# Three schedule changes around the start of the expert stage: a list prepared later in one part, one key chunk moved to VectorE, two rank products a gap later

## Chip, core and metric

The kernel runs on one NeuronCore of a Trainium2 chip. The metric is the device time of one execution in microseconds. Before the change three runs took 671.76 us (median), 670.19 and 672.02 us.

## What is computed

Three layers follow each other. Clustered attention (2 batches, 8 heads, 768 positions, 64 per head): a query sees only the keys of its own cluster, a key's or query's cluster being the nearest of 16 centroids. Its output, 1536 tokens of 512, goes through a mixture of 8 experts with two experts per token, and that through a soft mixture.

```python
mask = q_assign[:, :, :, None] == k_assign[:, :, None, :]
scores = np.where(mask, scale * np.matmul(q, k.transpose(0, 1, 3, 2)), -1e9)
attn = np.exp(scores - max) ; attn /= attn.sum(-1) + 1e-9 ; x = attn @ v
# experts: noisy top 2 of 8 per token
h = np.maximum(x[mask] @ w1[e], 0.0)            # 512 -> 1024
out[mask] += top2_w[mask, k, None] * (h @ w2[e])  # 1024 -> 512
# soft mixture: 32 slots, softmax over tokens in, over slots out
```

## The kernel before

Instructions are issued by hand in an order that Python loops write out; each engine then runs its own instructions in that order and waits for semaphores. Attention runs over 8 pairs of heads (NP = 8), each pair over two query halves `qh` and six key chunks `kc`. For each chunk TensorE makes the scores, ScalarE the exponentials `pt`, TensorE multiplies with the values. The denominators need the sum of the six `pt` tiles; `add` splits these sums: the first `n` chunks go to GpSimd (`psa`), the rest to VectorE (`psb`). `n` is 6 for pair 0, 4 below pair `MASKED` and 3 from it on.

The token routing is done by `gate`, called for the first 6 blocks of 128 tokens and then for two groups of 3. A gate is a list of some 40 small operations, most on VectorE, a few on ScalarE, and `rank`: a few small matmuls that number the tokens of each expert, followed by two VectorE operations that read the result. The integers in the list are pauses. `gap(s, n)` takes up to `n` operations off the list `todo`; an integer ends the gap, and counts down by one for each gap it ends. In the expert stage there are two gaps in each step, one after `first` and one after `second`, of 8 operations each. With the row numbers known, a scatter (`scatter`, L614, issued by GpSimd) writes rows of `x` to the list buffer `xg` in DRAM; the scatters of a group stand in `todo` behind or among the operations that follow.

The expert stage has 10 jobs of 8 steps: jobs 0, 1 and 8, 9 are short lists of 256 rows, jobs 2 to 7 long ones of 448. Step `s` is one eighth of an expert's hidden layer. In the loop over `s` the calls stand in this order: load the weights of step s+5 (`load_w`, SP's queue), at s = 9 empty `todo` and load the first long list (`load_x(2)`: four DMAs `xr<-xg` and three small ones `mt`), `first(s+1)` (12 matmuls `ph`, then `H` on ScalarE and its rounding remainder on VectorE), a gap, `second(s)` (matmuls `py`), a gap, `split_hi(s+3)` on ScalarE and `split_lo(s+3)` on VectorE (the weights as a rounded part and a remainder; in some short steps GpSimd makes half of the remainder), and then the preparation of the lists. After the last `second` of a job `evac` scales `y` and GpSimd adds its rows to `x2acc` by DMA (L893). The weights have four landing buffers `wr` and a ring of three split buffers. All loads named here stand in one queue, SP's, in the order of the loop.

A list is prepared by `prep_t` (VectorE transposes it), `prep_h` (ScalarE copies it rounded, `XS1a` for job 2) and `prep_l` (VectorE or GpSimd subtracts, `XS1b`). `PREP[2]` = (step, parts, engines) says where: part i is transposed in step 10 + i, and copied and subtracted one step later. Step 16, the first of job 2, needs all of it; its matmuls `first(16)` are issued in iteration 15.

Of the kernel before, what the change touches and what calls it, by code (L numbers as in the profile page):

```python
# [17 lines left out]
NP = B * H // 2  # L18
# [12 lines left out]
TRASH = NTOK  # L31
NTRASH = 512
XR = DM + 4
MASKED = NP - 2
TWO = 3
FF = 1024
NF = FF // 128
# [1 line left out]


OV = 24
PREP = {2: (10, 3, "ddd"), 4: (2, 3, "ppp"), 8: (3, 2, "dd"), 9: (8, 2, "dd")}
LOADS = {-16: ("b0",), -14: ("a0",), -12: ("a1",), -10: ("a2",), -8: ("a3",), -7: ("x0",), -6: ("x2",), -5: ("x4", "b2"), -4: ("b3",), -3: ("c0", "c1"), -2: ("c2", "c3")}
B4, B5, B6 = 8, 6, 4
X9 = 57
# [33 lines left out]
class Attention:  # L79
# [297 lines left out]
    def add(self, p, t):  # L377

        qh, kc = divmod(t, 6)
        pt = self.ptile  # L380
        n = 6 if p == 0 else 4 if p < MASKED else 3
        first = 0 if kc < n else n
# [66 lines left out]
class Dispatch:  # L449
# [63 lines left out]
    def gate(self, q, first, n):  # L513

        nc, g, xp = self.nc, self.g, self.g.xp
        b = first // (NCK // B)
# [26 lines left out]
        out = []  # L543

        def op(f, *a, **k):
            out.append(lambda: f(*[x() if callable(x) else x for x in a], **k))  # L546
# [35 lines left out]
        op(TTn, MB, oh[0], oh[1], op=OP.add)  # L582
        op(dv.reciprocal, wcol(1), lambda: t("ss", n))
        op(TTn, wcol(2), TT, wcol(1), op=OP.mult)
        out.append(3 if b == 0 else 1)

        def rank():
            ps = g.pm.tile([128, 512], F32, tag="misc", name="prank")
# [663 lines left out]
def body(tc, qk, q2, k2, v2, cent, wgn, noise, w12, phi, v12, out):  # L1252
    nc = tc.nc
    with ExitStack() as ctx:
# [211 lines left out]
        for j in range(2, len(M1.jobs)):  # L1466
            s, n, eng = PREP[j if j in PREP else 4]
            if j > 2:
# [127 lines left out]
```

## Time and profile before

| | before |
|---|---|
| runs, us | 670.19, 671.76, 672.02 |
| profiled execution, us | 670.41 |
| its span, first to last instruction, us | 668.6 |
| TensorE busy | 634.0 us (95%) |
| VectorE, ScalarE, GpSimd busy, us | 413.5, 314.4, 290.5 |
| mean granted TensorE clock | 0.982 |

The span is cut into attention (up to about 250 us), an overlap of attention's end with the first expert steps, the short jobs 0 and 1 with the last gates (to 311 us), the long jobs (to 559 us) and the rest. A row of a timeline reads: start, duration, engine, line, operation, tiles written and read, shapes, count, and in brackets the idle time before it and what ended that.

### The profile page before, as it was taken

The page shows a single profiled execution, that of the slowest core. Times are in us where ns is not written, and L with a number is a line of the kernel's source. Part 1 is how long each engine was busy: PE and PEld are TensorE (multiplying, and loading weights), DVE is VectorE, ACT ScalarE, POOL GpSimd, SP SyncE. Part 2 cuts the span into 40 slices and gives each one's busy share as a digit, 9 for nine tenths or more (in the row PEclk, how much of TensorE's full clock was granted, in tenths as well). Part 3 has the DMA queues.
Part 4 walks back from the last instruction along what each step waited for, and adds up shares of the span by engine and source line. Part 5 has one row for each costly group of instructions (what it writes and reads, how often), then busy time and mean ns, then how long its engine had stood idle before and what let it go on. Part 6 is the DMA issues. An engine that isn't in the chain of part 4 may idle for free. (4 is left out here: it accounts for less than half of the span.)

```text
span 668.6 us, 10904 instructions
## 1 busy us (share of the span) xinstructions
PE 634.0 (95%) x4004; PEld 485.8 (73%) x4004; DVE 413.5 (62%) x867; ACT 314.4 (47%) x446; POOL 290.5 (43%) x246
## 2 busy tenths in 40 slices
PE   7999999999798999778999999999999999997997
PEld 6556666676566668667888888888888888885544
DVE  5766889769766797737544544455544557645633
ACT  4676585675456562334334343344434336542102
POOL 4699586765678791661133141332413203101100
PEclk9799999999799999897999999999999999999999
DMA  7294753845537323595837559698793938988995
GB/s 303 73 240 133 253 194 116 281 140 182 185 111 259 83 98 119 185 239 204 184 122 149 155 173 270 235 288 297 221 329 127 214 125 247 309 293 283 385 395 191
DMA packets 63848, 140.31 MB, mean 210 GB/s; under 512 B 15344, under 2 KB 31536, under 8 KB 61744
## 3 DMA queue, kind: packets, MB, share of 16 engines
q1 hardware_dynamic: 57648, 125.64, 56.1%
q0 software_dynamic: 6144, 13.95, 9.7%
q8 instruction: 32, 0.52, 0.3%
q14 instruction: 24, 0.20, 0.1%
HBM read 108.51 MB, written 28.94 MB: 206 GB/s over the span
## 5 line engine op out<-in xcount | busy, mean ns | idle before, releaser
L885 PE MATMUL py<-ring,H 128*128 128x512 f32 x702 | 178.8, 399 | 6.0 <-DVE H L854 6.0
L758 DVE TENSOR_TENSOR ring<-wr,ring 128x1024 fp32r<-128x1024 f32 (+1 forms) x77 | 92.5, 1201 | 105.4 <-ACT ring L751 104.6
L885 PEld LDWEIGHTS py<-ring,H 128*128 128x128 f32 x702 | 131.2, 190 | 33.5 <-DVE H L854 6.6
L751 ACT ACTIVATE ring<-wr 128x1024 fp32r<-128x1024 f32 x77 | 81.6, 1059 | 96.7 <-PE py L885 78.8
L364 ACT ACTIVATE pt<-psc 128x768 f32<-128x768 f32 x96 | 77.2, 811 | 66.9 <-PE psc L361 56.8
L893 POOL DMA_INDIRECT x2acc<-y,mdi x32 | 49.7, 1552 | 114.0 <-ACT y L917 107.9
L851 ACT ACTIVATE H<-ph 128x448 fp32r<-128x448 f32 (+1 forms) x80 | 38.4, 479 | 78.8 <-PE ph L845 75.5
L374 PE MATMUL pav<-pt,vt 128*64 128x384 f32 x384 | 73.8, 506 | 0.0
L325 DVE TENSOR_REDUCE mp<-pmx 128x1 f32<-128x512 f32 x96 | 63.2, 675 | 16.9 <-PE pmx L320 16.2
L845 PE MATMUL ph<-XS1a,ring 128*128 128x448 f32 (+1 forms) x288 | 71.6, 338 | 0.8 <-DVE ring L758 0.8
L845 PE MATMUL ph<-XS0a,ring 128*128 128x448 f32 (+1 forms) x252 | 67.3, 348 | 1.6 <-DVE ring L758 1.4
L394 POOL TENSOR_TENSOR psa<-psa,pt 128x768 f32<-128x768 f32 x32 | 62.1, 1942 | 3.5 <-ACT pt L364 1.4
L854 DVE SCALAR_TENSOR_TENSOR H<-ph,H 128x384 fp32r<-128x384 f32 (+2 forms) x128 | 46.1, 392 | 27.5 <-ACT H L851 27.1
L845 PEld LDWEIGHTS ph<-XS1a,ring 128*128 128x128 f32 x288 | 48.6, 189 | 5.4 <-DVE ring L758 1.0
L845 PE MATMUL ph<-XS0b,ring 128*128 128x256 f32 (+1 forms) x192 | 49.6, 335 | 0.0
L845 PE MATMUL ph<-XS1b,ring 128*128 128x448 f32 (+1 forms) x192 | 48.5, 326 | 1.0 <-DVE ring L758 0.8
L845 PEld LDWEIGHTS ph<-XS0a,ring 128*128 128x128 f32 x252 | 43.8, 188 | 7.6 <-DVE ring L758 1.9
L814 POOL TENSOR_TENSOR XS0b<-xr,XS0a 128x640 fp32r<-128x640 f32 (+1 forms) x9 | 17.4, 1928 | 65.2 <-ACT XS0a L808 65.2
L374 PEld LDWEIGHTS pav<-pt,vt 128*64 128x64 f32 x384 | 23.6, 137 | 25.1 <-issue 19.7
L320 PE MATMUL pmx<-even 96*128 96x512 f32 (+1 forms) x96 | 32.5, 394 | 5.4 <-DVE mp L325 4.5
L330 DVE TENSOR_REDUCE mp<-pmx 128x2 f32<-128x512 f32 x48 | 33.0, 689 | 6.1 <-PE pmx L320 5.8
L614 POOL DMA_INDIRECT xg<-x,idx x24 | 26.0, 1082 | 23.7 <-DVE inv L546 17.8
(314 smaller groups left out, 1029.9 us busy)
## 6 DMA issues: line engine op xcount, KB each, us to landing
wr<-in_w SPq DMA_DIRECT2D x80, 512.0 KB
v<-in_v SPq DMA_DIRECT2D x9, 2048.0 KB
xg<-xr SPq DMA_DIRECT2D x14, 512.0 KB
wr<-in_qk SPq DMA_DIRECT2D x8, 768.0 KB
early<-in_q SPq DMA_DIRECT2D x8, 768.0 KB
early<-in_k SPq DMA_DIRECT2D x8, 768.0 KB
xr<-xg SPq DMA_DIRECT2D x24, 224.0 KB
x2acc<-xr SPq DMA_DIRECT2D x8, 512.0 KB
```

What stands on the lines that cost most here:

```text
L325: nc.vector.tensor_reduce(mp[:, 0, col:col + 1], ps, axis=AX.X, op=OP.max)
L330: nc.vector.tensor_reduce(mp[:, 1, c0:c0 + 2], ps.rearrange("p (a c) -> p a c", a=2), axis=AX.X, op=OP.max)
L364: nc.scalar.activation(pt, ps[:, :, :384], AF.Exp, scale=SCALE)
L374: nc.tensor.matmul(self.avp[p, qh][64 * hh:64 * hh + 64, :384], self.vt[p][:, hh, kc, :], pt[:, hh, :], start=(kc == 0), stop=(kc == 5))
L394: eng.tensor_tensor(s, s, pt.pop((p, t)), op=OP.add)
L751: self.nc.scalar.activation(self.ring[s][0], self.wr[s], AF.Copy)
L758: nc.vector.tensor_tensor(lo[:, :n], wr[:, :n], f32(hi)[:, :n], op=OP.subtract)
L845: nc.tensor.matmul(ph[:, :n], a[:, 128 * c:128 * c + 128], x[:, c, :], start=(c == 0 and i == 0), stop=(c == 3 and i == 2))
L851: nc.scalar.activation(HH, ph[:, :n], AF.Relu)
L854: nc.vector.scalar_tensor_tensor(o, ph[:, a:b], 0.0, f32(HH)[:, a:b], op0=OP.max, op1=OP.subtract)
L885: nc.tensor.matmul(o, x, y, start=(f == 0 and i == 0), stop=(f == NF - 1 and i == 2))
L893: st = nc.gpsimd.indirect_dma_start(out=out, out_offset=bass.IndirectOffsetOnAxis(ap=di, axis=0), in_=y, in_offset=None, compute_op=OP.add)
```

## The change

`MASKED` goes from 6 to 5: in the sixth pair (index 5) GpSimd sums chunks 0 to 2 and VectorE 3 to 5, as in the last two pairs before. `PREP[2]` goes from three parts in steps 10 to 12 to one part in step 13, so that its copy and its subtraction come in step 14. The pause ahead of `rank` in the last two gates ends two gaps and not one.

```diff
-MASKED = NP - 2
+MASKED = NP - 3
...
-PREP = {2: (10, 3, "ddd"), 4: (2, 3, "ppp"), 8: (3, 2, "dd"), 9: (8, 2, "dd")}
+PREP = {2: (13, 1, "d"), 4: (2, 3, "ppp"), 8: (3, 2, "dd"), 9: (8, 2, "dd")}
...
-        out.append(3 if b == 0 else 1)
+        out.append(3 if b == 0 else 2)
```

What this does to the order is seen on three engines. GpSimd first, where job 0's rows are added to `x2acc` and the last scatters to `xg` are issued (L760 is its half of a weight split; - is before, + the change):

```order
 L614 DMA xg<-x,idx 3712x516 x4
 L760 TENSOR_TENSOR ring<-wr,ring 128x512
+L614 DMA xg<-x,idx 3712x516 x2
+L892 MEMSET spacer 1x1
+L893 DMA x2acc<-y,mdi 2048x512
+L892 MEMSET spacer 1x1
+L893 DMA x2acc<-y,mdi 2048x512
 L614 DMA xg<-x,idx 3712x516 x6
-L892 MEMSET spacer 1x1
-L893 DMA x2acc<-y,mdi 2048x512
-L892 MEMSET spacer 1x1
-L893 DMA x2acc<-y,mdi 2048x512
```

The two additions of job 0 stood behind the last six scatters and stand ahead of them now.

VectorE before, from the transposes of the first part in step 10 to those of the second (L854 is the remainder of `H`, L758 the weight split, L801 `prep_t`, L814 `prep_l`; the number at a name tells one buffer from another):

```order
L801 STREAM_TRANSPOSE xr_93<-xr_93 128x512
L854 SCALAR_TENSOR_TENSOR H_2668<-ph_3164,H_2668 128x256
L758 TENSOR_TENSOR ring_2470<-wr_92,ring_2470 128x512
L814 TENSOR_TENSOR XS1b_91<-xr_93,XS1a_90 128x4x4x32
L801 STREAM_TRANSPOSE xr_93<-xr_93 128x640
L854 SCALAR_TENSOR_TENSOR H_2668<-ph_3192,H_2668 128x256
```

The first transposition stands ahead of the `H` that the step issues, here that of step 12. VectorE with the change, steps 13 to 15 (the splits are those of steps 16 and 17, the `H` those of steps 14, 15 and 16):

```order
L854 SCALAR_TENSOR_TENSOR H_2668<-ph_3213,H_2668 128x256
L758 TENSOR_TENSOR ring_2470<-wr_92,ring_2470 128x1024
L801 STREAM_TRANSPOSE xr_93<-xr_93 128x1792
L854 SCALAR_TENSOR_TENSOR H_2668<-ph_3238,H_2668 128x256
L758 TENSOR_TENSOR ring_2470<-wr_92,ring_2470 128x1024
L814 TENSOR_TENSOR XS1b_91<-xr_93,XS1a_90 128x14x4x32
L854 SCALAR_TENSOR_TENSOR H_2668<-ph_3264,H_2668 128x384
```

One transposition of 1792 columns now stands ahead of the `H` of step 15, and the subtraction directly ahead of the `H` of step 16. SP's queue has the same loads in the same order as before.

## Rows read from the trace of the kernel before

**Rows 1.** Stages: stretch, length, busy us of PE, PEld, DVE, ACT, POOL; clock; DMA share; GB/s.
```profile
296.50:302.50 6.00, 0.05 (x1) 0.00 (x0) 1.04 (x3) 0.30 (x1) 0.62 (x1) 0.89 1.14 272
302.50:307.50 5.00, 4.97 (x18) 4.49 (x19) 3.96 (x6) 2.53 (x5) 1.68 (x1) 0.50 0.61 235
361.30:555.00 193.70, 193.63 (x896) 167.33 (x897) 94.64 (x172) 79.15 (x105) 50.16 (x48) 1.00 0.74 219
```

**Rows 2.** Waits of TensorE from 262 to 340 us: total, times, longest.
```profile
PE py L885 <- DVE H L854: 6.0, 1, 6.0
PE prank L591 <- DVE mb L546: 2.6, 2, 2.1
```

**Rows 3.** Timeline of VectorE, ScalarE and TensorE, 300 to 313 us.
```profile
301.46 0.71 DVE L801 STREAM_TRANSPOSE xr<-xr 128x512 f32<-128x512 f32 x1 [7.79 <-DMA xr<-xg]
...
302.20 0.63 ACT L808 ACTIVATE XS1a<-xr 128x512 fp32r<-128x512 f32 x1 [6.44 <-DVE xr L801]
...
302.99 0.68 DVE L814 TENSOR_TENSOR XS1b<-xr,XS1a 128x512 fp32r<-128x512 f32 x1
303.59 0.84 DVE L801 STREAM_TRANSPOSE xr<-xr 128x640 f32<-128x640 f32 x1
...
304.69 1.06 ACT L751 ACTIVATE ring<-wr 128x1024 fp32r<-128x1024 f32 x1 [1.58 <-issue]
305.65 0.72 ACT L808 ACTIVATE XS1a<-xr 128x640 fp32r<-128x640 f32 x1
306.41 1.88 DVE L814 TENSOR_TENSOR XS1b<-xr,XS1a 128x640 fp32r<-128x640 f32 x1
...
310.18 1.23 DVE L758 TENSOR_TENSOR ring<-wr,ring 128x1024 fp32r<-128x1024 f32 x1 [0.83 <-ACT ring L751]
311.32 0.82 DVE L814 TENSOR_TENSOR XS1b<-xr,XS1a 128x640 fp32r<-128x640 f32 x1
...
312.19 0.47 PE L845 MATMUL ph<-XS1b,ring 128*128 128x448 f32 x1 [0.18 <-DVE XS1b L814]
```

**Rows 4.** Waits of SP's DMA queue, whole span.
```profile
SPq L769 <- DMA xg<-x,idx: 7.2, 1, 7.2
```

**Rows 5.** Timeline of SP, 290 to 300 us.
```profile
293.64 2.15 SPq L769 DMA_DIRECT2D xr<-xg  x4
```

**Rows 6.** Timeline of GpSimd, 280 to 293 us.
```profile
280.42 0.99 POOL L614 DMA_INDIRECT xg<-x,idx  x1 [4.32 <-DVE inv L546]
...
287.38 1.82 POOL L614 DMA_INDIRECT xg<-x,idx  x1 [0.30 <-issue]
...
289.51 1.56 POOL L893 DMA_INDIRECT x2acc<-y,mdi  x1 [0.23 <-POOL spacer L892]
...
291.38 1.59 POOL L893 DMA_INDIRECT x2acc<-y,mdi  x1 [0.27 <-DVE ring L758]
```

**Rows 7.** Timeline of the sixth pair's first half, 185 to 190 us.
```profile
186.91 0.62 DVE L441 TENSOR_TENSOR x<-px,rd 128x192 f32<-128x192 f32 x2 [0.45 <-PE px L438]
...
189.21 0.50 PE L320 MATMUL pmx<-even 96*128 96x256 f32 x2 [0.48 <-DVE mp L325]
```

**Rows 8.** VectorE's sums into psb from 150 to 260 us: count: ns min/median/max.
```profile
L394 DVE TENSOR_TENSOR psb<-psb,pt x4: 957/1680/2404, 215.0 to 253.1; 128x768 f32<-128x768 f32 x4
```

**Rows 9.** Timeline of TensorE, steps 6, 11 and 13.
```profile
277.18 2.82 PE L885 MATMUL py<-ring,H 128*128 128x512 f32 x6
...
293.11 1.55 PE L885 MATMUL py<-ring,H 128*128 128x512 f32 x6
294.50 1.59 PE L845 MATMUL ph<-XS0b,ring 128*128 128x256 f32 x12
```

**Rows 10.** Timeline of ScalarE, the scaling of job 0's rows.
```profile
283.22 0.69 ACT L917 ACTIVATE y<-py,mwt 128x512 f32<-128x512 f32 x1 [0.94 <-issue]
```

**Rows 11.** Last scatter of the first group (GpSimd), and the list loads behind it (SP).
```profile
216.02 0.97 POOL L614 DMA_INDIRECT xg<-x,idx  x1 [0.30 <-issue]
...
219.93 1.85 SPq L769 DMA_DIRECT2D xr<-xg  x4
```

## Prediction

> **What bounds the kernel now.** I read the stages first, then TensorE's waits, then the timeline around the longest of them, and last the waits of the queue that feeds it. In the long jobs TensorE is the bound: 193.63 of 193.70 us busy at full clock [rows 1]. So whatever delays the start of job 2 goes whole into the end, and the stretch before it is what the change can move. There TensorE waits once for 6.0 us, for VectorE's remainder of `H`, and twice for the rank products' input, 2.6 us together [rows 2].
>
> The 6.0 us lie between 296.5 and 302.5 us, where TensorE is busy 0.05 us. [...] VectorE did not do `H` because the transposition of the first list part stood ahead of it, and that had waited 7.79 us for `xr` [rows 3]. The list's load was issued at 293.64 [rows 5], after SP's queue had waited 7.2 us for scatters [rows 4]. The last scatter ended on GpSimd at 287.38 + 1.82 = 289.20 [rows 6]; so its data took 293.64 − 289.20 = 4.44 us more. The list landed at 301.46, 7.82 us after its issue began. The first matmul of job 2 that needs `XS1b` started at 312.19 [rows 3]. That time is my yardstick: from it on TensorE has no room to lose or gain.
>
> **The change part by part.** Durations are those of the one profiled execution; sums are made against its 670.41 us.
>
> *Sixth pair.* VectorE gets one addition more for each query half. The second half has idle time for it. In the first TensorE already waits 0.48 us for VectorE, and VectorE was idle only 0.45 us shortly before [rows 7]. The additions take 0.96 us at best, 1.68 in the median, 2.40 at worst [rows 8]. At 0.96 the path gets 0.96 − 0.45 = 0.5 later; at 2.40 it is 1.95. GpSimd's two spared additions save nothing: VectorE, not GpSimd, is the one waited for there. A gain is conceivable if the two engines slow each other less, so the lower bound is 0. I take +0.5, nearest to the row of the wait.
>
> *Rank products.* TensorE's 2.6 us of waiting go. Next late are the weight splits of those steps, which ScalarE issues behind small operations of the gates. I take −0.7; bounds −2.0 (nearly all of it) and +0.5 (nothing saved, and the operations behind the rank collide with splits). Job 0's rows are scaled at 283.22 + 0.69 = 283.91 [rows 10]; with +0.5 − 0.7 they are ready at 283.7.
>
> *GpSimd's order, the step that decides.* The six scatters started at 280.42 as soon as their row numbers were there, and the two additions to `x2acc` followed [rows 6]. With the change the additions stand ahead. They wait for job 0's rows, and the scatters wait behind them, although their row numbers are ready by then. The additions took 291.38 + 1.59 − 289.51 = 3.46 us, so they end at 287.2. After a pause of 0.3 the scatters follow. Before they took 289.20 − 280.42 = 8.78 us, two of the six being long ones; at the short pitch (0.97 + 0.30, five times, and a last 0.97) it would be 7.4. The middle of 294.9 and 296.3 is 295.6. The landing took 4.44; for the first group it took at most 219.93 − 216.99 = 2.94 [rows 11]. I take 3.7, the middle: **the list's load is issued at 299.3 instead of 293.64**. Bounds: 296.5 (rows ready at 282.4, short pitch, 2.94) and 301.4 (rows ready at 284.4, long pitch, 4.44).
>
> While the list's load waits in SP's queue, the weights of step 15 and later wait behind it. In the 4.44 us of the row other loads shared the DMA engines; here SP's queue will be empty of weights for some of that time. [...] No row of this trace isolates a scatter without other loads.
>
> *List and weights.* The list's four loads took 2.15 us to issue [rows 5]; 448 rows of 512 floats are 917 KB, and at the 272 GB/s of the stretch [rows 1] they last 3.4: 5.5 us at least, 7.82 at most as before. I take 6.5: landed at 305.8. The 512 KB of step 15's weights last 1.9 at the same rate: W = 307.7 (303.9 to 311.1).
>
> *TensorE up to there.* The stall in step 12 goes, since no transposition stands ahead of that `H` now. TensorE then runs on from 296.55 with the rest of second(12) (0.9) and then `first(14)` and `second(13)`, about 1.4 each (294.50 − 293.11 = 1.39 from one start to the next [rows 9]), and with −0.2 from the above it is at `first(15)` at about 300.1. GpSimd's half of a weight split, which stands behind the scatters now, delays this by some 0.5, inside what comes next. `first(15)` needs its weights split: W + 1.06 [rows 3] = 308.8. So TensorE stalls **about 8.5 us in place of 6.0**, and the clock will fall as it did in the rows after 301.
>
> *From W to job 2.* Splits 15 and 16 on ScalarE, with an `H` of 0.4 between: W + 2.5. VectorE's remainder of split 16, 1.23: W + 3.7. Transposition of 1792 columns: 0.71 for 512 and 0.84 for 640 [rows 3] give 0.13 per 128, and 2.0: W + 5.7. Beside it TensorE does `first(15)` and `second(14)` at half clock. `second` took 2.82 at half clock and 1.55 at full, and 1.59 for `first` becomes 2.9 in the same ratio [rows 9]; from W + 1.06 that ends at about W + 6.7. Only then is the ring buffer free for split 17: W + 7.7. `prep_h` behind it, 0.63 and 0.72 for 512 and 640 columns, makes 1.5 for 1792: W + 9.3. `prep_l`, 0.68 and 0.82 [rows 3], makes 2.1: W + 11.4 = **319.1**. Against 312.19 that is **+6.9**. At full clock it would be W + 9.4. The subtraction once took 1.88 for 640 columns [rows 3]; all of it at that rate would add 2.9.
>
> *Clock after that.* The second stall (for the subtraction) is about 5 us. I count nothing for it; another stretch as long as the 5 us at 0.50 [rows 1] would cost 2.5.
>
> Sum: 670.41 + 6.9 = 677.3 for an execution like the profiled one. The median of the runs is 1.35 above that one, so the forecast is 678.7. With all low ends and full clock: 303.9 + 9.4 = 313.3, +1.1. With the high ends: 311.1 + 11.4 + 2.9 = 325.4, +13.2.
>
> **Rivals.** *The list is not late (faster).* If the scatters are out early enough for the list's load to be issued by about 294.4 us, W + 9.4 is no later than 312.2 at full clock, and from there on the change gains. At best the load hinders nothing: TensorE is at `first(15)` at 300.1, `second(14)` ends at 302.9, and split 17, `prep_h` and `prep_l` (1.06 + 1.5 + 2.1) are done at 307.6, 4.6 earlier than 312.19. That gives 665.8, or 667.2 on the scale of the runs. For it: GpSimd had been idle 4.32 us ahead of the scatters [rows 6], the 6.0 us stall goes, and the rank waits go. Against it: the scatters now stand behind additions that can't start before 283, and six of them need at least 7.4 us. Also, even then the preparation in one part leaves TensorE idle for some 5 us.
>
> *The wait only changes place.* Scatters at the short pitch, quick landing and the clock back early: the low ends, +1.1, or 672.9, which is no difference that can be told. For it: most scatters did have the short pitch, and the first group landed within 2.94 [rows 11]. Against it: it needs all of them together, and a stall of over 4 us was followed by a half clock in the row that shows one.
>
> *Slow additions.* If VectorE's new additions take 2.40 [rows 8], all gets 1.5 later: 680.2. It is inside the forecast's range.
>
> **How the numbers follow.** Forecast (the load is late and job 2 starts late) 0.75, at 678.7, with 673.8 to 685.5 for its own terms; the wait that changes place 0.11; the list not late 0.14. About 0.3%, 2 us, is what a measurement of this kernel can tell from no change. So faster 0.14, same 0.11, slower 0.75. The range reaches down over the second rival and leaves the first out: 671.0 to 685.5.
>
> **What would show it.** On GpSimd the additions at about 284 and the last scatter ending at about 296; SP's list load issued at about 299 after a wait of over 10 us; no wait of TensorE for rank products and none in step 12; a wait of about 8 us ahead of `first(15)` and a second of 4 to 5 ahead of the first matmul with `XS1b`, at about 319; a clock near 0.5 between. In the sixth pair TensorE waits about 1 us instead of 0.48. I am wrong if the load is issued before 294.4, if TensorE isn't kept by the weights of step 15, or if `XS1b` is there before 312.

## The result and the profile after

Six runs of the changed kernel have a median of 680.81 us (678.82 to 683.44), six of the kernel before 671.89 (669.86 to 672.98). The ratio is 1.0146, 95% interval 1.0119 to 1.0173: 9.8 us slower by the ratio, 8.9 by the medians. The forecast was 678.7, in a range of 671.0 to 685.5, and 0.75 for slower.

The profiled execution took 683.44 us with a span of 681.7, so it stands 2.6 above its median, where that of before stood 1.5 below its own. Single executions also differ where the code is the same: by up to 5 us in when attention gets going, and behind the experts' last step, where no edit of this document changes anything, the rest took 66.7 us before and 70.7 after (66.3 to 71.0 over all traces used here). So positions in different traces are compared below by their distance to one matmul that stands ahead of everything the change touches, the first of the first gate's rank product (line 591). Here it is in the timeline of TensorE, first before and then after:

```profile
183.03 0.20 PE L591 MATMUL prank<-xr,tri 128*128 128x48 bf16 x1
```
```profile
181.20 0.20 PE L591 MATMUL prank<-xr,tri 128*128 128x48 bf16 x1
```

Attention comes first. TensorE's timeline after the change shows three waits for VectorE's maxima, where there was one of 0.48 us in this place [rows 7]:

```profile
188.96 0.51 PE L320 MATMUL pmx<-even 96*128 96x256 f32 x2 [2.06 <-DVE mp L325]
200.05 0.51 PE L320 MATMUL pmx<-even 96*128 96x256 f32 x2 [0.97 <-DVE mp L325]
206.29 0.50 PE L320 MATMUL pmx<-oddb 96*128 96x256 f32 x2 [1.41 <-DVE mp L325]
```

Behind the first and the third of them is the length of VectorE's two new additions, and what GpSimd does at that time (timelines of both engines after):

```profile
184.74 2.42 DVE L394 TENSOR_TENSOR psb<-psb,pt 128x768 f32<-128x768 f32 x1
202.25 2.40 DVE L394 TENSOR_TENSOR psb<-psb,pt 128x768 f32<-128x768 f32 x1
```
```profile
184.06 2.28 POOL L302 TENSOR_TENSOR even<-early,even 64x768 fp32r<-64x768 f32 x1 [10.34 <-ACT even L285]
201.19 2.63 POOL L292 TENSOR_TENSOR odda<-early,oddb 64x768 fp32r<-64x768 f32 x1 [3.18 <-ACT oddb L281]
```

Each addition ends 0.82 to 0.83 us after GpSimd's operation beside it (187.16 against 186.34, 204.65 against 203.82). The numbers fit an addition of 0.96 us [rows 8] that waited inside itself for GpSimd to be done; what ties the two engines is not shown. The second wait, of 0.97 us, has no addition ahead of it: VectorE and ScalarE both stand idle until 198.7 there. It is in every traced kernel with the sixth pair changed (0.94 to 1.00 us) and in none of the others; what makes it stays open.

Behind the first wait the granted clock fell, to 0.66 on average from 189 to 194 us. Two stages after, with the same columns as [rows 1]:

```profile
189.00:194.00 5.00, 5.00 (x18) 3.19 (x19) 2.02 (x4) 0.47 (x1) 4.46 (x5) 0.66 0.30 111
...
318.00:326.00 8.00, 6.68 (x24) 5.82 (x24) 2.18 (x4) 1.44 (x3) 0.00 (x0) 0.67 0.19 62
```

TensorE's waits from 262 to 340 us (total, times, longest) answer to [rows 2]:

```profile
PE ph L845 <- ACT ring L751: 7.7, 3, 4.8
PE ph L845 <- ACT XS1a L808: 2.8, 1, 2.8
PE ph L845 <- DVE ring L758: 2.3, 2, 1.5
PE ph L845 <- DVE XS1b L814: 1.3, 1, 1.3
```

The 6.0 us in step 12 and the 2.6 us for the rank products are gone. In their place TensorE waits for weight splits and for the list. GpSimd and SP answer to [rows 5, 6]; of six scatters the first and the last:

```profile
287.68 1.56 POOL L893 DMA_INDIRECT x2acc<-y,mdi  x1 [7.29 <-issue]
289.54 1.59 POOL L893 DMA_INDIRECT x2acc<-y,mdi  x1 [0.27 <-DVE H L854]
291.44 1.02 POOL L614 DMA_INDIRECT xg<-x,idx  x1 [0.30 <-issue]
...
298.08 0.98 POOL L614 DMA_INDIRECT xg<-x,idx  x1 [0.30 <-issue]
```
```profile
300.88 1.89 SPq L769 DMA_DIRECT2D xr<-xg  x4
```

The last scatter ended at 299.06 and the list's load was issued 1.82 us later. ScalarE, VectorE and TensorE from there on answer to [rows 3]:

```profile
308.75 1.06 ACT L751 ACTIVATE ring<-wr 128x1024 fp32r<-128x1024 f32 x1 [8.37 <-DMA wr<-in_w]
...
315.58 1.68 ACT L808 ACTIVATE XS1a<-xr 128x1792 fp32r<-128x1792 f32 x1
```
```profile
312.67 2.03 DVE L801 STREAM_TRANSPOSE xr<-xr 128x1792 f32<-128x1792 f32 x1
...
317.29 2.02 DVE L814 TENSOR_TENSOR XS1b<-xr,XS1a 128x1792 fp32r<-128x1792 f32 x1 [0.36 <-ACT XS1a L808]
```
```profile
302.21 1.46 PE L845 MATMUL ph<-XS0b,ring 128*128 128x256 f32 x10 [1.50 <-DVE ring L758]
...
309.86 3.23 PE L845 MATMUL ph<-XS0b,ring 128*128 128x256 f32 x12 [4.80 <-ACT ring L751]
...
317.31 0.74 PE L845 MATMUL ph<-XS1a,ring 128*128 128x448 f32 x1 [2.78 <-ACT XS1a L808]
319.37 0.74 PE L845 MATMUL ph<-XS1b,ring 128*128 128x448 f32 x1 [1.32 <-DVE XS1b L814]
```

The wait of 1.50 us is for VectorE's half of a weight split. It took 3.37 us beside GpSimd's two halves, which stand behind the scatters now, and 0.69 the next time (309.84):

```profile
298.79 3.37 DVE L758 TENSOR_TENSOR ring<-wr,ring 128x512 fp32r<-128x512 f32 x1 [1.64 <-ACT ring L751]
```
```profile
299.07 2.52 POOL L760 TENSOR_TENSOR ring<-wr,ring 128x512 fp32r<-128x512 f32 x2
```

ScalarE waits 8.37 us for the weights of step 15, TensorE 4.80 for their split, and the first matmul with `XS1b` starts at 319.37, which is 138.17 behind the common point; before it was 129.16. That is +9.0 us. From there to the experts' last step another 1.9 are lost: before, TensorE ran at full clock from 308 us on (stages of before below); now it ran at 0.67 from 318 to 326.

```profile
308.00:312.00 4.00, 4.00 (x24) 3.22 (x22) 3.17 (x5) 2.05 (x4) 0.00 (x0) 1.00 0.37 131
312.00:330.00 18.00, 17.82 (x83) 15.50 (x83) 9.61 (x21) 6.91 (x9) 3.17 (x3) 1.00 0.83 198
```

### The profile page after: what moved, and what is told of

Its sections match the earlier page's. It is cut to its first block, busy times and chain, and to the rows that moved or that the text cites. A ratio compares the mean times of both kernels' runs of the same rounds, so it can differ in the third digit from the quotient of the medians.

```text
span 681.7 us, 10900 instructions
## 1 busy us (share of the span) xinstructions
PE 638.9 (94%) x4004; PEld 487.3 (71%) x4004; DVE 419.7 (62%) x865; ACT 313.8 (46%) x444; POOL 286.2 (42%) x244
## 5 line engine op out<-in xcount | busy, mean ns | idle before, releaser
L758 DVE TENSOR_TENSOR ring<-wr,ring 128x1024 fp32r<-128x1024 f32 (+1 forms) x77 | 95.6, 1241 | 112.3 <-ACT ring L751 108.8
L845 PE MATMUL ph<-XS1a,ring 128*128 128x448 f32 (+1 forms) x288 | 73.1, 344 | 3.5 <-ACT XS1a L808 2.8
L854 DVE SCALAR_TENSOR_TENSOR H<-ph,H 128x384 fp32r<-128x384 f32 (+2 forms) x128 | 46.2, 392 | 32.8 <-ACT H L851 32.7
L394 POOL TENSOR_TENSOR psa<-psa,pt 128x768 f32<-128x768 f32 x30 | 58.5, 1951 | 3.4 <-ACT pt L364 1.4
L814 POOL TENSOR_TENSOR XS0b<-xr,XS0a 128x640 fp32r<-128x640 f32 (+1 forms) x9 | 17.3, 1926 | 65.2 <-ACT XS0a L808 65.2
L845 PEld LDWEIGHTS ph<-XS0b,ring 128*128 128x128 f32 x192 | 32.2, 200 | 13.6 <-ACT ring L751 7.9
L320 PE MATMUL pmx<-even 96*128 96x512 f32 (+1 forms) x96 | 33.1, 399 | 7.9 <-DVE mp L325 7.1
```

Of the source, the lines that this page charges most:

```text
L320: nc.tensor.matmul(o, self.BQ[i][:96, qh, hh, 128 * c:128 * c + 128], self.BK[i][:96, hh, ks], start=True, stop=True)
L394: eng.tensor_tensor(s, s, pt.pop((p, t)), op=OP.add)
L758: nc.vector.tensor_tensor(lo[:, :n], wr[:, :n], f32(hi)[:, :n], op=OP.subtract)
L845: nc.tensor.matmul(ph[:, :n], a[:, 128 * c:128 * c + 128], x[:, c, :], start=(c == 0 and i == 0), stop=(c == 3 and i == 2))
L854: nc.vector.scalar_tensor_tensor(o, ph[:, a:b], 0.0, f32(HH)[:, a:b], op0=OP.max, op1=OP.subtract)
```

## Experiments

Ratios are to runs of the kernel before that were made beside each kernel, with 95% intervals; 0.001 is 0.67 us. The table gives from each trace the distance in us from the common point to: the issue of the list's load, the split of the weights of step 15 where it waited for a DMA, the first matmul with `XS1b`, and the experts' last `second`. One execution of one kernel stands behind each row, and the clock falls in some of them and not in others, so a difference of 2 us in the last column is not much. In the two rows with the preparation in two parts, some 1.4 us of every distance were lost in attention already: both ran at a lower clock (0.50 from 212 to 214 us in each) behind a wait of 1.8 to 2.0 us that all kernels without the change to the sixth pair have there.

| kernel | ratio | list issued | split 15 | `XS1b` | last step |
|---|---|---|---|---|---|
| before | 1 | 110.6 | | 129.2 | 415.9 |
| sixth pair alone | 1.0060 (1.0032 to 1.0088) | 115.1 | | 134.6 | 421.1 |
| rank products alone | 1.0026 (0.9996 to 1.0056) | 113.9 | | 130.4 | 417.1 |
| preparation alone | 1.0075 (1.0048 to 1.0102) | 110.4 | 119.7 | 130.7 | 418.2 |
| all three: the change | 1.0146 (1.0119 to 1.0173) | 119.7 | 127.6 | 138.2 | 426.8 |
| without sixth pair | 1.0110 (1.0083 to 1.0138) | 115.5 | 123.3 | 135.1 | 423.3 |
| without rank products | 1.0114 (1.0082 to 1.0145) | 115.1 | 125.4 | 137.0 | 425.8 |
| without preparation | 1.0123 (1.0088 to 1.0158) | 119.6 | | 136.7 | 423.2 |
| change, additions behind scatters | 1.0147 (1.0112 to 1.0182) | 116.5 | 127.6 | 139.2 | 427.6 |
| change, weights 15 ahead of the list | 1.0141 (1.0111 to 1.0171) | 121.6 | | 137.6 | 424.8 |
| change, weights 15, 16 ahead | 1.0132 (1.0090 to 1.0175) | 121.9 | | 134.5 | 422.2 |
| preparation alone, weights 15, 16 ahead | 1.0018 (0.9991 to 1.0045) | 111.9 | | 126.4 | 416.1 |
| preparation in two parts | 1.0033 (1.0004 to 1.0062) | 112.6 | 122.0 | 132.2 | 420.3 |
| two parts, weights 15, 16 ahead | 1.0015 (0.9984 to 1.0047) | 114.0 | | 130.7 | 418.2 |

### Each part alone

```diff
-MASKED = NP - 2
+MASKED = NP - 3
```


> Only the sixth pair's split of the sums is changed. Theory M (read from the changed kernel's trace): VectorE's extra addition takes 2.4 us beside a GpSimd operation, TensorE stalls 2 us, its clock falls, and attention ends 4.2 us later; nothing behind takes it back, so 671.9 + 4.2 = about 676 us. Rival (the prediction's term): +0.5, about 672.4 us.

Measured: 4.0 us slower (0.0060 of 671.9; 2.1 to 5.9). Theory M holds, with list, `XS1b` and last step all 4.5 to 5.5 later. The prediction's +0.5 for this part was far too small.

```diff
-        out.append(3 if b == 0 else 1)
+        out.append(3 if b == 0 else 2)
```


> Only the pause ahead of the rank products is changed. Theory S: the additions of job 0 stand ahead of the last six scatters, the list's load is issued at about 298.5 us in place of 293.6, and since the preparation in three parts still hangs on it, the first matmul with XS1b comes about 5 us later: about 677 us. Rival R: what counts are the waits of TensorE for the rank products (2.6 us before), the scatters' delay is taken up elsewhere: 669 to 672 us.

Measured: 1.7 us slower, between the two, and with an interval that just takes in no change. The list was issued 3.3 us later, not 5, and the wait in step 12 grew. TensorE's waits from 262 to 340 us:

```profile
PE py L885 <- DVE H L854: 9.0, 1, 9.0
PE ph L845 <- ACT ring L751: 2.9, 2, 2.3
PE ph L845 <- DVE ring L758: 0.8, 1, 0.8
```

Two things are to be seen. The wait in step 12 is 3.0 longer than before, as long as the list is late; yet `XS1b` is only 1.2 later. Of the 3.3, some 1.2 came back since the list landed sooner after its issue (7.7 us to the matmul that waited, against 8.9), and 0.9 since the steps after the wait took 8.8 us and not 9.7. And the 2.6 us for rank products are replaced by waits for weight splits of 2.9 and 0.8 us, where there was one of 1.4 before. So in this trace the rank part gained nothing where it was made.

```diff
-PREP = {2: (10, 3, "ddd"), ...
+PREP = {2: (13, 1, "d"), ...
```


> Only the preparation is moved to step 13 in one part. Theory S: the 6.0 us stall in step 12 goes, but the weights of step 15, queued behind the list, land at about 301.5 us, first(15) waits for them, and from there it takes about 10.6 us to XS1b as in the changed kernel: 312 us as before, so 671 to 673 us, no change. Rival P: with the load on time the moved preparation gains what the prediction's faster case said, 4.6 us: about 667 us.

Measured: 5.0 us slower (3.2 to 6.8). Rival P falls. Theory S has the place right and the size too small. TensorE's timeline:

```profile
301.83 0.51 PE L845 MATMUL ph<-XS0b,ring 128*128 128x256 f32 x2 [3.57 <-ACT ring L751]
302.56 2.49 PE L845 MATMUL ph<-XS0b,ring 128*128 128x256 f32 x10 [0.22 <-DVE ring L758]
...
309.73 0.74 PE L845 MATMUL ph<-XS1a,ring 128*128 128x448 f32 x1 [2.78 <-ACT XS1a L808]
311.79 0.74 PE L845 MATMUL ph<-XS1b,ring 128*128 128x448 f32 x1 [1.32 <-DVE XS1b L814]
```

The list is on time here, and still TensorE waits 3.6 us ahead of `first(15)`, for weights that stand behind the list in SP's queue, and 4.1 ahead of job 2. Two waits, two falls of the clock, to 0.72 from 301.8 to 308 and lower behind the second, in job 2. A stage of this kernel:

```profile
308.00:316.00 8.00, 4.96 (x12) 4.07 (x13) 3.25 (x2) 1.67 (x2) 0.00 (x0) 0.59 0.24 86
```

`XS1b` is 1.6 later and the last step 2.3 in this trace; it is the fastest of the kernel's runs (672.18 of 672.18 to 678.61), and what the others lose beyond it was not traced.

### Each part left out of the change

The diffs are those above, backwards.

> The change without its part on the sixth pair. Theory: the attention's 4.0 us (measured alone) come back whole, since nothing behind takes them up: 680.8 - 4.0 = about 677 us. Rival: the scatters and the list's load pace what follows, whenever attention ends: 680 to 681 us.

> The change without its part on the rank products, so that the scatters stand ahead of job 0's additions again. Theory: the list's load is issued about 3.3 us earlier (296.97 against 293.64 in the traces of the rank part alone and of before), and the weights of step 15 and XS1b with it: about 677.5 us. Rival: TensorE is late there by what the preparation in one part takes, and only the rank part's own 1.7 us or less come back: 679 to 681 us.

Measured: 2.4 and 2.1 us less than the change (0.0036 and 0.0032, each with some 0.004 of uncertainty). Neither theory is told from its rival by the times alone. In the traces the list is issued 4.2 and 4.6 earlier, the split of step 15 is 4.3 and 2.1 earlier, `XS1b` 3.1 and 1.2. So the trace without the sixth pair sides with its theory; the one without the rank products does so for the list, but of that little more than 1 us reaches `XS1b`, as its rival said.

> The change without its part on the preparation. Theory: its cost is the sum of the other two alone (4.0 and 1.7), 5 to 6 us slower than before; the preparation's part brings the rest of the 9. Rival: with the list late, the preparation from step 10 on holds TensorE as long as the weights do in the changed kernel: 8 to 10 us slower than before.

Measured: 8.2 us slower than before (5.9 to 10.6). This fits the rival, and the theory's 5 to 6 lies at the edge of the interval. With list and scatters late, the preparation from step 10 on makes TensorE wait 8.9 us in step 12:

```profile
306.69 2.07 PE L885 MATMUL py<-ring,H 128*128 128x512 f32 x4 [8.91 <-DVE H L854]
```

By the ratios the sixth pair and the rank products together cost 8.2, more than their sum of 5.7, and the preparation adds 1.5 to them, where alone it costs 5.0. Each of these two differences has some 3.5 us of uncertainty, so neither is shown.

### GpSimd's order

```diff
-        self.add_rows(j, y, di[:p, m:m + 1], g.x2)
+        if j == 0:
+            self.later.append(lambda: self.add_rows(j, y, di[:p, m:m + 1], g.x2))
+        else:
+            self.add_rows(j, y, di[:p, m:m + 1], g.x2)
...
                     gap(1000, 1000)
+                for fn in M1.later:
+                    fn()
```


> All three parts of the change, but job 0's two additions to x2acc are issued behind the last scatters. Theory S: the scatters start when their row numbers are there, at about 285.6 us in place of 291.4, the list's load goes out some 5 us earlier, and 4 to 5 us come back: about 676 us. Rival: the position of the additions isn't on the path: 680 to 681 us.

Measured: 1.0147, as the change. The rival holds in the time, though the first half of the theory came true: the list was issued 3.2 us earlier. But the weights of step 15 were split at the same distance, 127.6. GpSimd's, SP's and ScalarE's timelines:

```profile
292.32 1.83 POOL L893 DMA_INDIRECT x2acc<-y,mdi  x1 [0.23 <-issue]
294.45 2.00 POOL L893 DMA_INDIRECT x2acc<-y,mdi  x1 [0.27 <-issue]
```
```profile
294.97 2.05 SPq L769 DMA_DIRECT2D xr<-xg  x4
```
```profile
306.01 1.06 ACT L751 ACTIVATE ring<-wr 128x1024 fp32r<-128x1024 f32 x1 [8.16 <-DMA wr<-in_w]
```

From the issue of the list to the split it took 11.0 us; in the changed kernel 7.9. The DMA view of that stretch (queue, packets, MB, share of the engines; q1 is SP's queue, q0 GpSimd's), first here (295 to 306 us) and then in the changed kernel (300.9 to 308.75), says what is different:

```profile
q1 hardware_dynamic: 2703, 2.00, 75.2%
q0 software_dynamic: 272, 0.49, 27.6%
```
```profile
q1 hardware_dynamic: 2655, 1.84, 95.7%
```

The additions' 0.49 MB now move beside the list, where they had been through before it. At the 227 GB/s of this stretch they would last 2.2 us, by estimate, of the 3.2 that it took longer. That they are the cause is argued from these two traces, not tested. In them the additions' place changed when the list could start, not when the weights were there.

### The order of SP's queue

`LX` is the step in which the list's load is queued; 10 lets the weights of step 15 go first, 11 those of 16 too.

```diff
-        LX = 9
+        LX = 10
```


> All three parts of the change, but on SP's queue the weights of step 15 stand ahead of the list's load, not behind it; GpSimd's order is the same. Theory Q (the list's load blocks the weights behind it): the wait of 4.8 us ahead of first(15) goes; XS1b is then set by the list's own landing (about 308.8 us) and its preparation (2.0 + 1.7 + 2.0 and small ones), about 315 in place of 319.4: 676 to 677 us. Rival: XS1b waits for the list in any case, and the wait only moves to first(16): 680 to 681 us.

Measured: 1.0141. The rival holds: the wait of 4.80 went, and that of 2.78 ahead of job 2 became 7.71. Now it is step 16's weights that stand behind the list, and their split waited for a DMA until 129.5. TensorE's timeline:

```profile
313.66 0.74 PE L845 MATMUL ph<-XS1a,ring 128*128 128x448 f32 x1 [7.71 <-ACT XS1a L808]
```

```diff
-        LX = 9
+        LX = 11
```


> All three parts of the change, with the weights of steps 15 and 16 ahead of the list's load. Theory Q: the list is issued at about the same time as in the changed kernel but first(15) and the splits don't wait; XS1b at about 313 to 314 in place of 319.4, 4 to 6 us less than the changed kernel, 4 to 5 us slower than before. Rival: as the changed kernel, 9 to 10 us slower than before.

Measured: 1.0132, 6.0 to 11.8 us slower than before. The interval takes in the rival's 9 to 10 and ends just above the 4 to 5 of theory Q. In the trace `XS1b` was 3.7 us earlier than in the change, near the 4 to 6 of theory Q, and the last step 4.6; the times don't show it. Why not stays open.

> The preparation in step 13 in one part alone (the rest as before the change), and on SP's queue the weights of steps 15 and 16 ahead of the list's load. Theory Q: no weights that TensorE needs stand behind the list; first(15) doesn't wait, and XS1b follows the list's landing (about 301.5 us) by 2.0 + 1.7 + 2.0 and small ones, at about 308 in place of 312.2: about 4 us faster than before. Rival: the same bytes go through the same DMA engines in that stretch, the list lands later by what stands ahead of it, and first(16) waits: as the part alone, 3 to 6 us slower than before.

Measured: 1.0018, no difference from before, and 3.8 us less than the preparation alone. Neither holds: `XS1b` came 2.7 us earlier than before, but the time didn't. TensorE's timeline and the stage behind it:

```profile
305.45 0.47 PE L845 MATMUL ph<-XS1a,ring 128*128 128x448 f32 x1 [4.16 <-ACT XS1a L808]
307.51 0.74 PE L845 MATMUL ph<-XS1b,ring 128*128 128x448 f32 x1 [1.59 <-DVE XS1b L814]
```
```profile
306.00:314.00 8.00, 6.49 (x19) 5.64 (x20) 2.15 (x3) 0.68 (x2) 0.00 (x0) 0.57 0.20 66
```

TensorE waits 5.75 us in all, as long as in step 12 before, and the clock falls behind it as before; only now it falls in job 2 instead of ahead of it. At 0.57 these 8 us hold 3.4 less of work, which is more than the 2.7.

> Preparation in two parts, transposed in steps 12 and 13, everything else as before the change. Theory S: no transposition stands in front of an H that TensorE waits for; first(15) waits about 2.5 us for its weights (landed at about 301.5), and XS1b is ready some 7 us behind these, at about 308.5 in place of 312.2: about 668 us. Rival: the stall is set by the list's landing and only moves: 671 to 673 us.

> The same queue order with the preparation in two parts (steps 12 and 13). Theory Q: the second part's copy and subtraction are shorter (0.9 and 1.0 us), XS1b at about 306.5, some 5 us faster than before. Rival: as the two parts alone, 1 to 4 us slower than before.

The diffs are `PREP[2] = (12, 2, "dd")`, and the same with `LX = 11`. Measured: 2.2 and 1.0 us slower. In both cases theory Q or S expected 4 to 5 us less than before, and both fall. The intervals (0.3 to 4.2 slower, and 1.1 faster to 3.2 slower) overlap with the ranges of their rivals. No version that was tried is faster than the kernel before.

## Why the prediction was right

The sign, the time and the order of events were right. Two terms were mis-sized, the weight given to one step was too great, and part of the agreement is luck: errors up to the scatters are partly cancelled by errors behind them. The table gives both as distances from the common point (for the prediction its positions less 183.03):

| | predicted | measured | later by |
|---|---|---|---|
| job 0's rows scaled on ScalarE | 100.7 | 105.7 | 5.0 |
| additions ended | 104.2 | 109.9 | 5.8 |
| last scatter ended | 112.6 | 117.9 | 5.3 |
| list's load issued | 116.3 | 119.7 | 3.4 |
| weights of step 15 split | 124.7 | 127.6 | 2.9 |
| first matmul with `XS1b` | 136.1 | 138.2 | 2.1 |

In the trace's own times 319.37 stands against 319.1; that they are so close is chance, since this execution reached the common point 1.83 us sooner.

**Sixth pair: mis-sized.** +0.5 was predicted (0 to 1.95) and 4.0 measured, alone. The prediction took the addition at 0.96, the shortest row, though [rows 8] had 1.68 and 2.40 beside it, and held the second query half's to be hidden; it took 2.40 too. Its rival of slow additions had the 2.40 right but counted 1.5 for it. Of the 4.2 us by which attention is later at the first expert steps, three waits are 4.4 in place of 0.5 and 2.0; most of the rest is the clock behind the first of them (5 us at 0.66 lose 1.7).

**Rank products: gain not there.** −0.7 was predicted (−2.0 to +0.5). The waits for ranks went as said, and those for splits took their place, as the prediction feared. Job 0's rows were ready 4.8 us later than before, 4.2 of it from attention.

**List's load: 3.4 later than predicted, two errors against each other.** The additions ended 5.8 later; 0.8 of that is VectorE's part of the scaling (286.95 to 287.70), at whose end the first addition started (287.68) and which the prediction left out. But the scatters kept the short pitch (7.6 against 8.1), and the list's load was issued 1.82 us behind the last of them, below the lower bound of 2.94. The prediction took 3.70 and pointed to SP's queue, empty of weights for some of that time. No run here isolates that. In the traces the time goes with GpSimd's order: it was 1.82 to 1.83 us in three with the additions ahead of the scatters (the change, the rank products alone, without the sixth pair), and 2.95 to 4.44 in six with them behind. In the changed kernel 0.26 MB of GpSimd's queue moved in that time and nothing of SP's; before it was 0.79 MB and 0.39. The cause may be what GpSimd's own queue still has to move; that is argued from these numbers, not tested.

**Stalls.** The wait ahead of `first(15)` was 4.80 and 1.50 ahead of the step before, where about 8.5 was predicted for the one: TensorE came later itself. Of the 1.50 the prediction had 0.5, for GpSimd's half of the split. Ahead of job 2 it was 4.1 (4 to 5 predicted). From the split to the matmul with `XS1b` it took 10.6 (11.4 predicted), with 2.03, 1.68 and 2.02 for the three operations (2.0, 1.5, 2.1). The 0.8 less is `second(14)`, which ran in 1.65 us from 312.88, at a clock of 0.95, where the prediction had it at half clock (2.82).

**Clock.** The prediction took it that TensorE has nothing to lose behind `XS1b`, and counted nothing after job 2's start; 1.9 were lost there, within the 2.5 named.

**Range.** Its upper end is 0.5 above what its own high ends give: 670.41 + 13.2 + 1.35 = 685.0. Nothing hangs on it.

**What the runs add: no step decides alone.** The prediction called GpSimd's order "the step that decides", and its faster rival put the turning point at the issue of the list's load. Both are wrong as a cause. With the scatters ahead again nothing comes back, and with the list on time and nothing else changed the kernel is 5.0 slower, not 4.6 faster. What this rival had wrong lies behind the issue: in that trace it was 9.3 us from there to the split of step 15's weights (8.4 in the prediction's sum), and 11.1 from the split to `XS1b`, where the rival counted 9.4 at full clock; TensorE waited 3.6 us for the split, and its clock fell (0.50 from 304 to 306 us). Its best case left out these weights altogether. Each part alone costs 4.0, 1.7 and 5.0, each known to about 2 us and the second not told from nothing; each left out gives back 2.4, 2.1 and 1.5, each known to some 3 us.

## What to carry to other kernels

A wait that hides another can't be priced alone: moving the list's preparation took away 6.0 us in step 12 and showed the wait for weights behind it, in a queue that the change didn't touch. Where work moves from GpSimd to VectorE, take its duration from rows where GpSimd is busy at that time (2.40 us here), not from the shortest (0.96). And look for a lower clock behind a wait of TensorE, wherever that then falls. Here it was 0.50 for 5 us behind the 6.0 us before the change, and in the changed kernel 0.50 for 3 us behind the 4.80 (309.86 to 312.88) and 0.67 from 318 to 326, where the 4.1 ahead of job 2 ends. With the preparation alone it was 0.59 from 308 to 316, where such a 4.1 ends, and with weights 15, 16 ahead of the list as well 0.57 from 306 to 314, where 5.75 end.

## What the runs showed of the hardware

An addition of 0.96 us on VectorE took 2.40 to 2.42 when it started while GpSimd was inside a tensor operation, and ended 0.82 to 0.83 behind that operation's end, twice. At 217.26 and 255.45 us of the same trace, the changed kernel's, it took 0.96, with GpSimd in no tensor operation. What ties the two engines is not shown.

Behind a wait of about 2 us of TensorE in attention (L320) the clock was lower in some executions and not in others. Behind 2.06 us in the changed kernel it was 0.66 on average for 5 us; behind 1.99 before the change it stayed at 1.00 (212.7 to 217). Of two kernels with the same code up to there, both with a wait of 1.97 us, one stayed at 1.00 (preparation alone, weights 15, 16 ahead; 210 to 216) and the other fell to 0.50 (two parts, weights 15, 16 ahead; 212 to 214).

The load that waits for GpSimd's last scatter was issued 1.82 us after the scatter's end on the engine in the changed kernel, where GpSimd's queue moved 0.26 MB in that time and SP's nothing. Before the change it was 4.44 us, with 0.79 MB and 0.39; with the additions behind the scatters it was 2.95, and 3.75 without the rank products.
